# Giving the last unit's products banks of their own, folding the other sums in ahead, and writing the output through four banks

## The chip, the cores and the metric

One core of one Trainium2 chip. The metric is the device time of one execution in microseconds (us); the lower the better. The executions of the kernel before lie between 2330.62 and 2333.46 us, so they scatter by 2.8 us. TensorE, VectorE, ScalarE (ACT), GpSimd (POOL) and SyncE (SP) are the engines; SP issues all transfers of the output.

## The reference

```python
# x, f_logit: (4, 6080, 256); lower_bound: (256,)
f = lower_bound + (1 - lower_bound) * sigmoid(f_logit)
h = f[:, t] * h + (1 - f[:, t]) * x[:, t]      # for each t; y[:, t] = h
# y as (24320, 256); w_in (256, 2048), w_out (2048, 256)
h = y @ w_in
out = (h - tanh(h)) @ w_out
```

## The kernel before

The tokens run in blocks of 512, the hidden layer in four units of 512. Both matrix products use a seven-product scheme of the Strassen kind: in the second layer, the seven products of a unit accumulate over the units in four PSUM banks (pieces of the memory that TensorE writes its products to), Qa to Qd, and at the end of a block they are added up into the four quadrants C of the output. For all blocks but the last, that happens beside the next block's work. For the last there is nothing beside it, and its own routine `end` is used. The fast path is only valid for small values. It leaves a flag, and every engine reads the flag and branches around a general path.

```python
PARTS = (
    (("Qa", 0, A11, "h", 0), ("Qa", 1, S1, "T", 0)),
    (("Qb", 0, A12, "h", 3), ("Qb", 1, S2, "h", 1)),
    (("Qc", 0, S3, "T", 1),),
    (("Qd", 0, S4, "h", 2), ("Qd", 1, A22, "T", 2)),
)
...
def finish(j, step):          # p15 copies Qa; o1 to o4 add up C
...
    o, a, b = (
        None,
        (C[:, 0:2], acc[j, 1][:, :, 0:hb], twice(0)),
        (C[:, 2], acc[j, 2][:, 0, 0:hb], C[:, 1]),
        (C[:, 1:4:2], C[:, 1:3], twice(1)),
        (C[:, 1:3], acc[j, 3][:, :, 0:hb], C[:, 1:3]),
    )[step]
    nc.vector.tensor_tensor(out=o, in0=a, in1=b, op=ALU.add)
...
def end(j):                   # the last block, in place of o4
...
    for half in range(2):
        slot, r = ((2, 1), (1, 0))[half]
        nc.vector.tensor_tensor(
            out=C[:, slot], in0=acc[j, 3][:, r, 0:hb], in1=C[:, slot], op=ALU.add
        )
        name = ("Qa", "Qb")[half]
        bank = ps_b.tile([P, 2, KC, P], FP32, name=name, tag=name)
        for i in range(2):
            for k in range(KC):
                nc.tensor.transpose(
                    bank[:, i, k], C[:, 2 * k + half, i * P : (i + 1) * P], ident[:]
                )
        rows = osb[:, 2 * half : 2 * half + 2]
        (nc.scalar.copy, nc.vector.tensor_copy)[half](
            out=rows.rearrange("p i (m k) -> p i k m", k=KC), in_=bank[:]
        )
        t0 = starts[j] + half * hb
        nc.sync.dma_start(
            out=out[t0 : t0 + hb, :].rearrange("(i p) d -> p i d", p=P), in_=rows
        )
...
fast()
seen = nc.values_load(flag[:].bitcast(INT32), ...)
with tc.If(seen != 0):
    general()
```

Of the kernel before, what the change touches and what calls it, by code (L numbers as in the profile page):

```python
# [9 lines left out]
FP32 = mybir.dt.float32  # L10
ALU = mybir.AluOpType
# [6 lines left out]
P = 128  # L18
# [13 lines left out]
def kernel(  # L32
# [25 lines left out]
    nc = tc.nc  # L58

    B, S, D = x.shape  # L60
    DFF = moe_w_in.shape[1]
    N = B * S
    KC = D // P
    TB = 512
    HB = TB // 2
    NQ = TB // P
    NU = DFF // TB
# [6 lines left out]
    sizes = [HB] + [TB] * (N // TB)  # L74
    PLAIN, TURNED = 2, 2
    starts = [sum(sizes[:j]) for j in range(len(sizes))]
    NBLK = len(starts)
# [11 lines left out]
    ident = const.tile([P, P], FP32, name="ident")  # L89
# [156 lines left out]
    def fast(ctx):  # L246
# [11 lines left out]
        mixpool = ctx.enter_context(tc.tile_pool(name="mix", bufs=2))  # L258
# [6 lines left out]
        ps_a = ctx.enter_context(tc.tile_pool(name="ps_a", bufs=2, space=PSUM))  # L265
        ps_b = ctx.enter_context(tc.tile_pool(name="ps_b", bufs=1, space=PSUM))
# [4 lines left out]
        w_out = [wpool.tile([P, 7, 2 * P], FP32, name=f"w_out{u}") for u in range(NU)]  # L271
        A11, S3, A12, A22, S1, S2, S4 = range(7)
# [44 lines left out]
        def sum_weight(kind, u, s3):  # L317
            w = (w_in, w_out)[kind][u]
            A21 = S3
            sums = (  # L320
                (S1, A21, A22, ALU.add),
                (S2, S1, A11, ALU.subtract),
                (S4, A12, S2, ALU.subtract),
            )
            for o, a, b, op in ((S3, A11, A21, ALU.subtract),) if s3 else sums:
                nc.vector.tensor_tensor(
                    out=w[:, o, :], in0=w[:, a, :], in1=w[:, b, :], op=op
                )
# [126 lines left out]
        acc = {}  # L455

        def second_layer(n, part):


            j, u = units[n]  # L460
            products = PARTS[part]
            if u == 0:
                acc[j, part] = ps_b.tile([P, 2, HB], FP32, name=products[0][0])
            for c in range(2):
                for _, r, slot, right, q in products:
                    nc.tensor.matmul(  # L466
                        acc[j, part][:, r, 0 : st[n]["hb"]],
                        lhsT=w_out[u][:, slot, c * P : (c + 1) * P],
                        rhs=piece(n, right)[:, q, c],
                        start=(u == c == r == 0),  # L470
                        stop=(u == NU - 1 and c == 1),
                        skip_group_check=True,
                    )

        def finish(j, step):



            hb = sizes[j] // 2
            if step == 0:  # L480
                acc[j, "p"] = sumpool.tile([P, 2, HB], FP32, name="p15")
                nc.scalar.copy(out=acc[j, "p"][:, :, 0:hb], in_=acc[j, 0][:, :, 0:hb])
                return
            if step == 1:
                acc[j, "C"] = sumpool.tile([P, 4 * HB], FP32, name="C")
            C = acc[j, "C"][:, 0 : 4 * hb].rearrange("p (n t) -> p n t", n=4)

            def twice(i):
                return acc[j, "p"][:, i : i + 1, 0:hb].broadcast_to([P, 2, hb])
# [10 lines that stand above are left out]
        def give(j):  # L500
# [11 lines left out]
            for i in range(G):  # L512
# [2 lines left out]
                    in_=osb[i * H : (i + 1) * H, 0:n],  # L515
                )

        def end(j):


            hb = sizes[j] // 2
            C = acc[j, "C"][:, 0 : 4 * hb].rearrange("p (n t) -> p n t", n=4)
            osb = opool.tile([P, NQ, D], FP32, name="osb", tag="osb")
            for half in range(2):
                slot, r = ((2, 1), (1, 0))[half]
                nc.vector.tensor_tensor(
                    out=C[:, slot], in0=acc[j, 3][:, r, 0:hb], in1=C[:, slot], op=ALU.add
                )
                name = ("Qa", "Qb")[half]
                bank = ps_b.tile([P, 2, KC, P], FP32, name=name, tag=name)  # L530
                for i in range(2):
                    for k in range(KC):
                        nc.tensor.transpose(
                            bank[:, i, k], C[:, 2 * k + half, i * P : (i + 1) * P], ident[:]
                        )
                rows = osb[:, 2 * half : 2 * half + 2]
                (nc.scalar.copy, nc.vector.tensor_copy)[half](
                    out=rows.rearrange("p i (m k) -> p i k m", k=KC), in_=bank[:]
                )
                t0 = starts[j] + half * hb  # L540
                nc.sync.dma_start(
                    out=out[t0 : t0 + hb, :].rearrange("(i p) d -> p i d", p=P), in_=rows
                )

        steps.update(
# [14 lines left out]
            Qa=lambda n: second_layer(n, 0),  # L560
            Qb=lambda n: second_layer(n, 1),
            Qc=lambda n: second_layer(n, 2),
            Qd=lambda n: second_layer(n, 3),
# [6 lines left out]
            p15=lambda j: finish(j, 0),  # L570
            o1=lambda j: finish(j, 1),
            o2=lambda j: finish(j, 2),
            o3=lambda j: finish(j, 3),
            o4=lambda j: finish(j, 4),
            otr=give,
# [24 lines left out]
        for word in around.split():  # L600
            name, u, at = re.fullmatch(r"([a-zA-Z0-9]+)(?:\.(\d))?([+-]\d)?", word).groups()
# [156 lines left out]
        def p_give(j):  # L758
# [26 lines left out]
            A=lambda kind, u: sum_weight(kind, u, False),  # L785
            B=lambda kind, u: sum_weight(kind, u, True),
            F=p_first,
            t=p_square,
            q=p_quadratic,
            a=p_factor,  # L790
# [3 lines left out]
            o=p_give,  # L794
# [42 lines left out]
        def sum_up():  # L837

            most = ps_b.tile([P, 2, HB], FP32, name="most", tag="D")
            nc.tensor.matmul(  # L840
                most[0:1, 0, 0:1], lhsT=worst[:], rhs=ones[:], start=True, stop=True
            )
            nc.scalar.copy(out=flag[:], in_=most[0:1, 0, 0:1])
# [24 lines left out]
        def open_by(words):  # L868
            for word in words:
                name, *at = word.split(".")  # L870
                at = [int(i) for i in at]
                if name in opening:
                    opening[name](*at)
                else:
                    steps[name](at[0] * NU + at[1] if len(at) == 2 else at[0])

        with tc.manual_schedule():
            nc.vector.memset(zeros[:], 0.0)
            nc.vector.memset(ones[:], 1.0)
            nc.scalar.dma_start(  # L880
                out=lb[:], in_=lower_bound.rearrange("(p k) -> p k", k=KC)
            )
            make_identity(nc, ident[:])

            nc.scalar.activation(out=flag[:], in_=ones[0:1, :], func=AF.Sigmoid)
            nc.scalar.activation(
                out=om[:], in_=lb[:], func=AF.Identity, scale=-1.0, bias=1.0
            )
            nc.scalar.activation(out=nom[:], in_=lb[:], func=AF.Identity, bias=-1.0)
            busy = ps_b.tile([P, TB], FP32, name="B", tag="B")  # L890
            open_by(before.split())
            for cycle in range(PLAIN + 1, NBLK + 3):
                for name, u, at in turns:
                    j = cycle + at
                    if not PLAIN <= j < NBLK:
                        continue
                    if u is None:
                        if (name, j) == ("o1", NBLK - 1):
                            nc.vector.reduce_max(
                                out=worst[:], in_=flags[:], axis=mybir.AxisListType.X  # L900
                            )
                        if j == NBLK - 1 and name in ("o4", "otr"):
                            if name == "o4":
                                end(j)
                            continue
                        if (name, j) == ("o3", NBLK - 1):
                            sum_up()
                        steps[name](j)
                        if name == "tx" and j + 1 < NBLK:
                            fetch(j + 1)  # L910
                        continue
                    steps[name](j * NU + u)

    @with_exitstack
    def general(ctx):
# [15 lines left out]
        with tc.manual_schedule():  # L931
# [12 lines left out]
            for j, nb in enumerate(sizes):  # L944
# [57 lines left out]
                )  # L1002

    fast()
    seen = nc.values_load(
        flag[:].bitcast(INT32),
# [36 lines left out]
```

## Time and profile before

| | before |
|---|---|
| time, median of 3 runs (range) | 2332.53 us (2331.93 to 2333.46) |
| span of the profiled execution | 2329.3 us |
| end of TensorE's last product, by its pass's record | 2322.11 us |
| issues of the two output transfers | 2323.85 and 2324.43 us |
| last landing of the second | 2328.18 us |

The trace has 16 landings for each of these transfers; I take them as the reports of the 16 transfer engines that each write a part, and count the transfer as done with the last of them.

To compare ends of kernels, I count time in the rest of this document from one instruction that all of them have: the start of the one-column product `most`, which makes the flag. In the timeline of the kernel before it is this line (start, duration, engine, line, operation):

```profile
2319.99 0.19 PE L840 MATMUL most<-ones,worst 128*1 128x1 f32 x2
```

A time counted so is written with a plus sign. The span of the kernel before ends at +9.32.

### The profile page before, as it was taken

The numbers are of one execution on the slowest core, as the hardware profiler recorded it, in microseconds if no ns is written. First come the engines' busy times: TensorE is split into PE (matmuls) and PEld (weight loads), VectorE is DVE, ScalarE is ACT, GpSimd is POOL, SyncE is SP. The second block draws the span as 40 slices with busy tenths as digits, with TensorE's granted clock in tenths as the row PEclk, the third lists the DMA queues.
The fourth block names the chain that finished last, engine by engine and source line by source line (L and its number), as shares of the span: only waits on it lengthen the run. The fifth ranks groups of instructions, "written<-read, shape, count | busy, mean of one in ns | idle before, by whom it ended". The sixth has DMA issues, their size and how long they took to land.

```text
span 2329.3 us, 28648 instructions
## 1 busy us (share of the span) xinstructions
PE 2319.6 (100%) x10677; PEld 2025.2 (87%) x10677; DVE 2121.4 (91%) x2447; ACT 1801.1 (77%) x2686; POOL 0.7 (0%) x6
## 2 busy tenths in 40 slices
PE   9999999999999999999999999999999999999998
PEld 6888888888888888888888888888888888888887
DVE  8999899998999989999999999999899998999987
ACT  7677777777777777787777777777777777777775
POOL 0000000000000000000000000000000000000000
PEclk9999999999999999999999999999999999999999
DMA  6311211111111111112111121111211112111101
GB/s 172 64 24 32 42 37 28 28 35 39 37 28 28 37 36 37 28 28 42 32 37 28 28 45 28 37 28 28 46 29 36 28 28 46 31 33 28 28 10 29
DMA packets 296932, 85.05 MB, mean 37 GB/s; under 512 B 289872, under 2 KB 292688, under 8 KB 296784
## 3 DMA queue, kind: packets, MB, share of 16 engines
q1 hardware_dynamic: 296640, 83.14, 16.9%
q8 instruction: 85, 1.39, 0.2%
q14 instruction: 63, 0.52, 0.1%
q10 hardware_dynamic: 144, 0.00, 0.0%
HBM read 58.20 MB, written 24.90 MB: 36 GB/s over the span
## 4 chain that ended last, share of the span: by engine, by line
PE 99%; DMA 0%; SPq 0%; DVE 0%; issue 0%
PE A L383 27%; PE Qd L466 14%; PE Qa L466 14%; PE Qb L466 14%; PE D L383 14%; PE Qc L466 7%; PE B L383 7%; PE Qc L749 1%; PE Qb L749 1%; PE Qa L749 1%; PE A L682 1%; PE D L682 0%; PE Qd L682 0%; DMA xn<-in_x_dram 0%; PE B L682 0%; PE Qc L682 0%
## 5 line engine op out<-in xcount | busy, mean ns | idle before, releaser
L383 PE MATMUL A<-T,w_in 128*128 128x256 f32 x2208 | 558.8, 379 | 0.0
L383 PEld LDWEIGHTS A<-T,w_in 128*128 128x128 f32 x2208 | 419.5, 190 | 57.0
L427 DVE TENSOR_TENSOR h<-h,q 128x1024 f32<-128x1024 f32 x368 | 437.7, 1220 | 3.1
L421 DVE SCALAR_TENSOR_TENSOR q<-q,t 128x1024 f32<-128x1024 f32 x368 | 440.2, 1217 | 0.0
L414 ACT ACTIVATE q<-t 128x1024 f32<-128x1024 f32 x368 | 382.8, 1053 | 46.3 <-DVE h L427 43.4
L411 ACT ACTIVATE t<-h 128x1024 f32<-128x1024 f32 x368 | 388.7, 1057 | 3.1 <-DVE h L398 0.3
L432 ACT ACTIVATE junk<-t 128x1024 bf16<-128x1024 f32 x368 | 388.2, 1055 | 1.5
L446 DVE TENSOR_TENSOR Tg<-h 128x1024 f32<-128x1024 f32 x368 | 348.1, 946 | 6.4
L466 PE MATMUL Qb<-h,w_out 128*128 128x256 f32 x1472 | 347.7, 379 | 0.0
L466 PEld LDWEIGHTS Qb<-h,w_out 128*128 128x128 f32 x1472 | 279.7, 190 | 38.0
L466 PE MATMUL Qa<-Tg,w_out 128*128 128x256 f32 x736 | 219.0, 379 | 0.0
L466 PE MATMUL Qd<-h,w_out 128*128 128x256 f32 x736 | 219.0, 379 | 0.0
L466 PE MATMUL Qa<-h,w_out 128*128 128x256 f32 x736 | 218.9, 379 | 0.0
L466 PE MATMUL Qd<-Tg,w_out 128*128 128x256 f32 x736 | 218.9, 379 | 0.0
L395 ACT COPY h<-B 128x512 f32<-128x512 f32 x184 | 107.0, 582 | 143.2 <-PE B L383 94.4
L395 ACT COPY h<-A 128x512 f32<-128x512 f32 x184 | 107.3, 583 | 136.7 <-PE A L383 125.3
L398 DVE TENSOR_TENSOR h<-D,r 128x512 f32<-128x512 f32 x184 | 126.9, 690 | 92.9 <-PE D L383 90.8
L398 DVE TENSOR_TENSOR h<-A,r 128x512 f32<-128x512 f32 x184 | 126.3, 687 | 74.3 <-PE A L383 42.5
L395 ACT COPY r<-A 128x512 f32<-128x512 f32 x184 | 107.3, 583 | 105.9 <-PE A L383 105.9
L383 PE MATMUL D<-y,w_in 128*128 128x256 f32 x736 | 188.9, 379 | 0.0
L383 PE MATMUL B<-y,w_in 128*128 128x256 f32 x736 | 188.9, 379 | 0.0
L383 PE MATMUL A<-y,w_in 128*128 128x256 f32 x736 | 188.9, 379 | 0.0
(120 smaller groups left out, 3069.8 us busy)
## 6 DMA issues: line engine op xcount, KB each, us to landing
xn<-in_x_dram SPq DMA_DIRECT2D x184, 128.0 KB, 3.2
fn<-in_f_logit_dram SPq DMA_DIRECT2D x184, 128.0 KB, 3.1
out_dram<-osb SPq DMA_DIRECT2D x180, 128.0 KB, 2.8
raw<-in_moe_w_in_dram SPq DMA_DIRECT2D x8, 512.0 KB, 4.6
raw<-in_moe_w_out_dram SPq DMA_DIRECT2D x8, 512.0 KB, 4.8
out_dram<-osb SPq DMA_DIRECT2D x3, 256.0 KB, 3.7
fn<-in_f_logit_dram SPq DMA_DIRECT2D x1, 512.0 KB, 6.9
xn<-in_x_dram SPq DMA_DIRECT2D x1, 512.0 KB, 7.7
```

What stands on the lines that cost most here:

```text
L383: nc.tensor.matmul(ps[:, c], lhsT=w_in[u][:, slot, c * P : (c + 1) * P], rhs=mixes[j][right], start=start and c == 0, stop=True, skip_grou ...
L395: nc.scalar.copy(out=dst, in_=piece(n, bank))
L398: nc.vector.tensor_tensor(out=piece(n, "h")[:, q], in0=piece(n, bank), in1=piece(n, r), op=ALU.add)
L411: nc.scalar.activation(out=half(n, i, "t"), in_=half(n, i), func=AF.Square)
L414: nc.scalar.activation(out=half(n, i, "q"), in_=half(n, i, "t"), func=AF.Square, scale=RA, bias=RB,)
L421: nc.vector.scalar_tensor_tensor(out=q, in0=q, scalar=RC, in1=t, op0=ALU.add, op1=ALU.mult)
L427: nc.vector.tensor_tensor(out=h, in0=h, in1=q, op=ALU.mult)
L432: nc.scalar.activation(out=junk[:, :, :, 0 : st[n]["hb"]], in_=t, func=AF.Relu, bias=-TINY, accum_out=flags[:, 2 * n + i : 2 * n + i + 1],)
L446: nc.vector.tensor_tensor(out=o, in0=a, in1=b, op=ALU.subtract)
L466: nc.tensor.matmul(acc[j, part][:, r, 0 : st[n]["hb"]], lhsT=w_out[u][:, slot, c * P : (c + 1) * P], rhs=piece(n, right)[:, q, c], start=( ...
L682: nc.tensor.matmul(h[c], lhsT=w_in[u][:, 2 * k + s, c * P : (c + 1) * P], rhs=ys[j][:, k, 0:nb], start=k == 0 and (c == 0 or len(banks) == 2),
L749: nc.tensor.matmul(acc[j][i // 2][:, i % 2].rearrange("p (k m) -> p k m", k=2), lhsT=plain[j, u][:, s, c, i * P : (i + 1) * P], rhs=w_out[ ...
```

## The change

The intent: the last additions wait for all of Qd although each needs half of it (the first starts at 2322.14, Qd's last pass ends at 2322.11), and the copies and transfers wait for whole halves. In the kernel before, the passes (single runs of TensorE) of Qd's two products alternate. The change also puts the passes (single runs of TensorE) of each product together, the one that is needed first ahead. So the last unit's two Qd products go into banks of their own (`alone`), what Qd holds of the other three units is copied out early and folded into C ahead (`kept`), and each half of the output passes through two banks, which ACT and VectorE copy at the same time.

```diff
--- before.py
+++ after.py
@@ -515,31 +515,67 @@
                     in_=osb[i * H : (i + 1) * H, 0:n],
                 )
 
+        def part_end(j, step):
+            hb = sizes[j] // 2
+            p, kept = acc[j, "p"][:, :, 0:hb], acc[j, "kept"]
+            if step == "o1":
+                finish(j, 1)
+            if step == "p15":
+                nc.vector.tensor_tensor(
+                    out=kept[:, 2], in0=p[:, 1], in1=kept[:, 0], op=ALU.add
+                )
+                return
+            C = acc[j, "C"][:, 0 : 4 * hb].rearrange("p (n t) -> p n t", n=4)
+            for o, a, b in {
+                "o1": (),
+                "o2": ((kept[:, 3], acc[j, 2][:, 0, 0:hb], C[:, 1]),),
+                "o3": (
+                    (C[:, 2], kept[:, 3], kept[:, 1]),
+                    (C[:, 1], C[:, 1], kept[:, 2]),
+                    (C[:, 3], kept[:, 3], p[:, 1]),
+                ),
+            }[step]:
+                nc.vector.tensor_tensor(out=o, in0=a, in1=b, op=ALU.add)
         def end(j):
 
 
-            hb = sizes[j] // 2
+            hb, n = sizes[j] // 2, j * NU + NU - 1
             C = acc[j, "C"][:, 0 : 4 * hb].rearrange("p (n t) -> p n t", n=4)
             osb = opool.tile([P, NQ, D], FP32, name="osb", tag="osb")
+            alone = [ps_a.tile([P, TB], FP32, name="A", tag="A")[:, 0:hb] for _ in range(2)]
+            for half, (slot, right, q) in enumerate(((A22, "T", 2), (S4, "h", 2))):
+                for c in range(2):
+                    nc.tensor.matmul(
+                        alone[half],
+                        lhsT=w_out[NU - 1][:, slot, c * P : (c + 1) * P],
+                        rhs=piece(n, right)[:, q, c],
+                        start=c == 0,
+                        stop=c == 1,
+                    )
             for half in range(2):
-                slot, r = ((2, 1), (1, 0))[half]
+                slot = 2 - half
                 nc.vector.tensor_tensor(
-                    out=C[:, slot], in0=acc[j, 3][:, r, 0:hb], in1=C[:, slot], op=ALU.add
-                )
-                name = ("Qa", "Qb")[half]
-                bank = ps_b.tile([P, 2, KC, P], FP32, name=name, tag=name)
+                    out=C[:, slot], in0=alone[half], in1=C[:, slot], op=ALU.add
+                )
                 for i in range(2):
-                    for k in range(KC):
+                    name = ("Qa", "Qb", "Qc", "D")[2 * half + i]
+                    bank = ps_b.tile([P, KC, P], FP32, name=name, tag=name)
+                    for k in (0, 1) if half == 0 else (1, 0):
                         nc.tensor.transpose(
-                            bank[:, i, k], C[:, 2 * k + half, i * P : (i + 1) * P], ident[:]
+                            bank[:, k], C[:, 2 * k + half, i * P : (i + 1) * P], ident[:]
                         )
-                rows = osb[:, 2 * half : 2 * half + 2]
-                (nc.scalar.copy, nc.vector.tensor_copy)[half](
-                    out=rows.rearrange("p i (m k) -> p i k m", k=KC), in_=bank[:]
-                )
+                    (nc.scalar.copy, nc.vector.tensor_copy)[i](
+                        out=osb[:, 2 * half + i].rearrange("p (m k) -> p k m", k=KC),
+                        in_=bank[:],
+                    )
                 t0 = starts[j] + half * hb
                 nc.sync.dma_start(
-                    out=out[t0 : t0 + hb, :].rearrange("(i p) d -> p i d", p=P), in_=rows
+                    out=out[t0 : t0 + hb, :].rearrange("(i p) d -> p i d", p=P),
+                    in_=osb[:, 2 * half : 2 * half + 2],
                 )
 
         steps.update(
@@ -894,22 +930,35 @@
                     j = cycle + at
                     if not PLAIN <= j < NBLK:
                         continue
+                    final = j == NBLK - 1
+                    if final and (name, u) == ("Qd", NU - 1):
+                        continue
                     if u is None:
-                        if (name, j) == ("o1", NBLK - 1):
+                        if final and name == "o1":
                             nc.vector.reduce_max(
                                 out=worst[:], in_=flags[:], axis=mybir.AxisListType.X
                             )
-                        if j == NBLK - 1 and name in ("o4", "otr"):
-                            if name == "o4":
-                                end(j)
+                        if final and name == "o3":
+                            sum_up()
+                        if final and name == "o4":
+                            end(j)
+                        if final and name[0] == "o":
+                            if name in ("o1", "o2", "o3"):
+                                part_end(j, name)
                             continue
-                        if (name, j) == ("o3", NBLK - 1):
-                            sum_up()
                         steps[name](j)
                         if name == "tx" and j + 1 < NBLK:
                             fetch(j + 1)
+                        if final and name == "p15":
+                            part_end(j, name)
                         continue
                     steps[name](j * NU + u)
+                    if final and (name, u) == ("Qd", NU - 2):
+                        kept = mixpool.tile([P, 4, HB], FP32, name="T")
+                        acc[j, "kept"] = kept
+                        nc.scalar.copy(
+                            out=kept[:, 0:2], in_=acc[j, 3][:, :, 0 : sizes[j] // 2]
+                        )
 
     @with_exitstack
     def general(ctx):
```

## The prediction

> **What bounds the kernel now.** I read the page's busy times first, then the chain of work that ended last, then the timeline of the last ten microseconds, because the diff touches only the last block.
>
> ```profile
> PE 2319.6 (100%) x10677; PEld 2025.2 (87%) x10677; DVE 2121.4 (91%) x2447; ACT 1801.1 (77%) x2686; POOL 0.7 (0%) x6
> PE 99%; DMA 0%; SPq 0%; DVE 0%; issue 0%
> ```
>
> TensorE is busy for the whole span and makes 99% of the chain. A change of a few instructions can only matter where TensorE has nothing left to do, which is after its last product. The chain in order of time shows where that is:
>
> ```profile
> 2317.47 1.73 PE Qb L466 x8
> 2319.20 0.86 PE Qc L466 x4
> 2320.06 0.12 PE most L840 x2
> 2320.18 1.94 PE Qd L466 x8
> 2322.14 0.43 DVE C L526
> 2322.62 0.55 PE Qa L533 x3
> 2323.17 0.52 PE Qb L533 x4
> 2323.71 0.69 DVE osb L537
> ```
>
> The last products (Qd, eight passes of 0.216 us) end at 2322.11. Then come, one after another, an addition, seven transposes, a copy of 512 columns and the output transfers. The span is 2329.3, so everything after the last product is 7.2 us, 0.3% of it. That is the ceiling of any gain here, and most of it is not compute: the transfers and the end of the program take the last 4.9 us. The timeline:
>
> ```profile
> 2320.56 0.69 DVE L498 TENSOR_TENSOR C<-C,p 128x512 f32<-128x512 f32 x1
> 2322.14 0.76 DVE L526 TENSOR_TENSOR C<-Qd,C 128x256 f32<-128x256 f32 x2 [0.89 <-PE Qd L466]
> 2322.62 0.55 PE L533 MATMUL Qa<-ident,C 128*128 128x128 f32 x3 [0.41 <-DVE C L526]
> 2323.21 0.61 ACT L537 COPY osb<-Qa 128x512 f32<-128x512 f32 x1 [2.84 <-PE Qa L533]
> 2323.71 0.69 DVE L537 COPY osb<-Qb 128x512 f32<-128x512 f32 x1 [0.81 <-PE Qb L533]
> 2323.85 0.97 SPq L541 DMA_DIRECT2D out_dram<-osb  x2
> ```
>
> The reader is to see that VectorE idles 0.89 us for Qd, TensorE then 0.41 us for VectorE, and that the two transfers go out at 2323.85 and 2324.43 (two issues of 0.39 within 0.97). The lines of the output transfers and of the branch at the program's end say what follows:
>
> ```profile
> DMA to landing us min/median/max: 3.7/3.7/3.8
> L1009 PEldq COMPARE_BRANCH  x1: 3711/3711/3711, 2323.7 to 2323.7; - x1
> L1009 DVEq EVENT_SEMAPHORE  x1: 21/21/21, 2327.6 to 2327.6; - x1
> ```
>
> So the second transfer lands at 2324.43 + 3.75 = 2328.18, and 1.14 us later the span ends. TensorE takes 3.71 us to get past the branch around the general path, until 2327.37, and VectorE resumes at 2327.6: these are 0.6 us behind the landing, not far. The landings of the two transfers show one thing more. On 15 of the 16 engines the first transfer has landed by 2326.59 and the second by 2327.56, most of them by 2325.95 and 2326.70; one engine is last for both, at 2327.57 and 2328.18. Instruction fetches (two of 8 KB at 2324.60 and 2324.66, one of 16 KB at 2324.71 that takes 1.24 us) run just as the output packets start, and that straggler is what sets the end.
>
> [...]the addition that needs only half of Qd starts at 2322.14, after all eight passes (2322.11). This is why the change gives each product its own bank.[...] The trace has 424 and 691 or 692 for the additions of C. So splitting an operation in two costs a fixed part again; though two independent ones overlap (L526 starts at 2322.145 and 2322.486, 0.34 apart).[...]
>
> **The change, part by part.** The instruction orders of the two kernels differ in nothing but the last block's end.
>
> First, the sums. The copy of Qd after the third unit (ACT, 512 columns, about 0.57 us) lands in the 5.20 us in which ACT waits for Qa, and the addition of kept and p (0.42 us on VectorE) in the gap of 0.72 us before L498 at 2319.30. Both are hidden: 0. The fold-in then puts three additions of 256 columns in the place of one of 512: started at 2320.56, then 2320.90 and 2321.24. The first needed addition of the last product follows at 2321.58, where the old one started at 2322.14, provided its product is ready. It is: the first product's four passes take the place of the first four of Qd and end at 2321.24.
>
> Second, the transposes. The addition ends at 2322.00. TensorE does the other product until 2321.94, so it meets the finished C with hardly a wait: Qa's second transpose at 2322.06 (before 2322.62), Qb's two at 2322.22 and 2322.33 (0.165 after the first, then 0.109, as in the trace). TensorE work is the same: eight passes and eight transposes.
>
> Third, the copies, now of 256 columns in four banks. ACT copies Qa from 2322.42 for 0.40 (L762 has 0.40 for such a copy). VectorE copies Qb from 2322.64 to 2323.06. The first transfer is issued at **2323.09, 0.76 us earlier** than 2323.85.
>
> Fourth, the second half, and here is the catch. In VectorE's order the second addition stands behind the copy of Qb, though its product is ready at 2322.11. It starts at 2322.64 + 0.34 = 2322.98 and ends at 2323.40. The last transposes of Qc and D follow at 2323.45, 2323.61 and 2323.72, end at 2323.99, and VectorE's copy of D runs 2324.03 to 2324.45. The second transfer is issued at **2324.47, against 2324.43 before: 0.04 us later.** What the copies' halving wins (0.27 us) and what the early addition wins is spent in VectorE's queue.
>
> Fifth, the landing. The first transfer's 16 KB per engine takes 16 packets of 46 ns, 0.74 us, so it leaves the engines before about 2324.8, when the second's packets are not yet there. The straggler then carries only one output transfer behind the fetches. The branches move later by 0.3 to 0.6 us with the last waits of each engine, so the fetches still meet the second transfer. If the straggler spends 1.36 us on fetches (2324.60 to 2325.96) from about 2325.0 and then 0.74 on the packets, it is done at 2327.1, against 2327.77 before, and lands at about 2327.5. But TensorE and VectorE come out of the branch at about 2327.8, 0.4 us later than before with some of it given back by freer engines. The later of the two, near 2327.8, stands against 2328.18.
>
> The sum: 0 (hidden sums) + 0.04 (issue) − 0.44 (landing, limited by the fetches) = −0.4 us. From 2332.53 this makes **2332.1 us**.
>
> **The rivals.** (a) The full gain: 0.76 us, if the second half followed the first as it does on ACT. Against it stands VectorE's order. It would make 2331.8. (b) No gain: the second issue is where it was, and if the straggler owes its delay to fetches alone, which move later with the branches, the landing stays or slips by 0.3 us. It would make 2332.5 to 2332.8.[...] (c) VectorE becomes the bound of the end earlier: three additions end at 2321.66 instead of 2321.25. The old addition waited until 2322.14 in any case, so this has 0.5 us of slack; I give it little. (d) A wait on another bank, say of a transpose for the copy of the flag (2320.37) or of the kept sums, is long over and costs nothing.
>
> **Range and chances.** All rivals lie within 1 us, 0.04% of the time. The three runs before span 1.5 us, which is larger than the effect, so the range is mostly noise: 2331.1 to 2333.1. A change of 2% would be 47 us, and the whole part that the diff touches lasts about 10 us, so within 2% is nearly certain.
>
> **What would show each step right or wrong.** The timeline after should show: the first addition of the last product near 2321.6; no wait of TensorE above 0.15 us before Qa's second transpose; the first issue near 2323.1 and the second near 2324.5; the second addition starting after the copy of Qb, not at 2322.14; landing of the second transfer 3.0 to 3.4 us after its issue instead of 3.75. I am wrong if the second issue comes before 2324.0 (then VectorE's order did not bind), if the second transfer still takes 3.7 us or more to land (rival b), or if TensorE shows a new wait before its last products.

## The result, and the profile after

| | before | changed |
|---|---|---|
| time, median of 6 runs (range) | 2332.3 us (2331.25 to 2333.46) | 2332.8 us (2331.64 to 2333.39) |
| ratio | 1 | 1.0001 (95% interval 0.9988 to 1.0014) |
| span of the profiled execution | 2329.3 us | 2330.3 us |
| first, second issue of output | +3.85, +4.44 | +3.43, +4.52 |
| TensorE reaches the branch, gets past it | +3.66, +7.37 | +4.04, +8.31 |
| last landing of the second transfer | +8.19 | +8.46 |
| end of the span | +9.32 | +9.59 |

A ratio here is the mean time of one kernel's runs over that of the other's of the same rounds, so it is not quite the ratio of the medians.

The profiled span is 1.0 us longer, but most of that is not the end of the kernel. The product `most` starts at 2320.74 instead of 2319.99, and up to the last products the two kernels have the same instructions in the same order on every engine but for two early sums (a copy on ACT and an addition on VectorE). The difference is there in the first 20 us. From the view of stretches, TensorE alone, before and then changed (stretch, its length, TensorE busy, instructions, granted clock, share of the transfer engines, GB/s):

```profile
0.00:10.00 10.00, 6.83 (x19) 1.00 0.79 255
10.00:20.00 10.00, 9.53 (x44) 1.00 1.17 292
```

```profile
0.00:10.00 10.00, 6.67 (x19) 1.00 0.77 236
10.00:20.00 10.00, 8.78 (x43) 1.00 1.12 291
```

TensorE is busy 16.36 us of them before and 15.45 after. In the fourteen profiles `most` starts anywhere from 2319.80 to 2322.33, with no visible relation to what was changed at the end. The changed kernel's two profiles show what this does to the time: of the 1.26 us between their spans, 0.94 lies before `most` and 0.32 after it.

The end itself, from the timeline of the changed kernel:

```profile
2320.74 0.19 PE L876 MATMUL most<-ones,worst 128*1 128x1 f32 x2
...
2321.31 0.42 DVE L541 TENSOR_TENSOR C<-T 128x256 f32<-128x256 f32 x1
...
2322.32 0.42 DVE L561 TENSOR_TENSOR C<-A,C 128x256 f32<-128x256 f32 x1
...
2323.16 0.38 ACT L571 COPY osb<-Qa 128x256 f32<-128x256 f32 x1 [2.04 <-PE Qa L568]
...
2323.38 0.42 DVE L571 COPY osb<-Qb 128x256 f32<-128x256 f32 x1 [0.64 <-PE Qb L568]
2323.72 0.41 DVE L561 TENSOR_TENSOR C<-A,C 128x256 f32<-128x256 f32 x1
2324.17 1.48 SPq L576 DMA_DIRECT2D out_dram<-osb  x2
...
2324.19 0.33 PE L568 MATMUL Qc<-ident,C 128*128 128x128 f32 x1 [0.74 <-DVE C L561]
...
2324.78 0.42 DVE L571 COPY osb<-D 128x256 f32<-128x256 f32 x1 [0.64 <-PE D L568]
```

The first addition starts at +1.58 (2322.32 minus 2320.74) instead of +2.15, as intended. The second starts at +2.98 instead of +2.49, because in VectorE's order it stands behind the copy of Qb, and that waits 0.64 us for TensorE. TensorE in turn waits 0.74 us for the second addition. The two issues of the output, 0.39 us each, stand 1.09 apart within the 1.48 of their line. The chain of waits of the changed kernel names the same step, between VectorE's copy and the last transposes:

```profile
2323.38 0.42 DVE osb L571
2323.80 0.34 DVE C L561
2324.14 0.04 issue
2324.19 0.33 PE Qc L568
```

And this is what follows the issues, from the lines of the transfers and of the branch in the changed kernel:

```profile
DMA to landing us min/median/max: 2.8/3.4/3.9
L1058 PEldq COMPARE_BRANCH  x1: 4267/4267/4267, 2324.8 to 2324.8; - x1
L1058 DVEq EVENT_SEMAPHORE  x1: 21/21/21, 2329.0 to 2329.0; - x1
```

The first transfer now lands 2.8 us after its issue (3.7 before), but the second needs 3.9 instead of 3.75, and TensorE's branch comes 0.4 us later and takes 4.27 us instead of 3.71.

### The profile page after: what moved, and what is told of

It is laid out like the page before. It is cut to its first block, busy times and chain, and to the rows that moved or that the text cites. A ratio compares the mean times of both kernels' runs of the same rounds, so it can differ in the third digit from the quotient of the medians. Undisturbed runs are those within 1.5% of the kernel's fastest.

```text
span 2330.3 us, 28654 instructions
## 1 busy us (share of the span) xinstructions
PE 2319.4 (100%) x10677; PEld 2025.3 (87%) x10677; DVE 2122.1 (91%) x2451; ACT 1802.2 (77%) x2688; POOL 0.7 (0%) x6
## 4 chain that ended last, share of the span: by engine, by line
PE 99%; DMA 0%; SPq 0%; DVE 0%; issue 0%
PE A L383 27%; PE Qa L466 14%; PE Qb L466 14%; PE D L383 14%; PE Qd L466 14%; PE B L383 7%; PE Qc L466 7%; PE Qa L785 1%; PE Qb L785 1%; PE Qc L785 1%; PE A L718 1%; PE D L718 0%; PE Qd L718 0%; DMA xn<-in_x_dram 0%; PE B L718 0%; PE A L552 0%
## 5 line engine op out<-in xcount | busy, mean ns | idle before, releaser
L383 PE MATMUL D<-T,w_in 128*128 128x256 f32 x736 | 188.9, 379 | 0.0
```

The costliest lines, as they stand in the source:

```text
L383: nc.tensor.matmul(ps[:, c], lhsT=w_in[u][:, slot, c * P : (c + 1) * P], rhs=mixes[j][right], start=start and c == 0, stop=True, skip_grou ...
```

## The experiments

The theories. **Q**: VectorE's queue order holds the second half back. **D**: the end follows the issue of the second output transfer. **F**: the end follows the branch, whose instruction fetches (packets of the kind "instruction" in the trace) hold up one engine of the output transfers and the engines that take the branch. Line numbers differ from kernel to kernel by a few. All twelve runs were correct.

| run | issues | TensorE at and past branch | last landing | end | ratio to before (interval) |
|---|---|---|---|---|---|
| before | +3.85, +4.44 | +3.66, +7.37 | +8.19 | +9.32 | 1 |
| before_again | +3.86, +4.44 | +3.67, +7.32 | +8.13 | +9.27 | 0.9999 (0.9979 to 1.0019) |
| changed | +3.43, +4.52 | +4.04, +8.31 | +8.46 | +9.59 | 1.0001 (0.9988 to 1.0014) |
| after_again | +3.43, +4.52 | +4.04, +7.83 | +7.98 | +9.27 | 0.9999 (0.9983 to 1.0016) |
| add_first | +3.42, +3.93 | +3.22, +7.23 | +8.08 | +9.21 | 0.9993 (0.9976 to 1.0010) |
| two_banks | +3.29, +4.05 | +3.23, +7.70 | +8.52 | +9.65 | 0.9998 (0.9982 to 1.0015) |
| four_banks_only | +4.00, +5.10 | +4.62, +8.85 | +9.08 | +10.21 | 1.0001 (0.9984 to 1.0017) |
| per_half | +3.11, +3.78 | +3.23, +7.62 | +8.44 | +9.57 | 0.9999 (0.9983 to 1.0016) |
| before_late_branch | +3.86, +4.44 | +5.36, +9.28 | +7.57 | +10.40 | 1.0004 (0.9988 to 1.0021) |
| before_late_transfer | +3.86, +5.16 | +3.67, +8.08 | +8.77 | +10.01 | 1.0008 (0.9991 to 1.0025) |
| before_nobranch | +3.85, +4.44 | none | +6.79 | +7.80 | 0.9995 (0.9978 to 1.0012) |
| after_nobranch | +3.43, +4.52 | none | +6.67 | +7.69 | 0.9994 (0.9977 to 1.0010) |
| add_first_nobranch | +3.42, +3.93 | none | +6.34 | +7.36 | 0.9993 (0.9977 to 1.0010) |
| per_half_nobranch | +3.11, +3.78 | none | +6.04 | +7.06 | 0.9990 (0.9973 to 1.0007) |

No total time is clear of noise: every interval holds 1. What follows is read from the traces, mostly one profile for each kernel, and a difference of less than 0.3 us at the end is not counted, since the changed kernel's two profiles differ by that (+9.59 and +9.27).

### How far the ends repeat

The changed kernel and the kernel before once more, with no edit.

> The changed kernel once more, for how far the profile of the end repeats. Second transfer issued at +4.52 (plus or minus 0.05, it is a fixed chain of compute), its landing and the end within 0.3 us of +8.46 and +9.59. The first transfer is issued 0.33 us after VectorE's copy of the second bank has ended; whether this repeats is open. The opening (time of 'most' from the start of the span, 2319.99 before and 2320.74 in the changed kernel) should scatter by about 0.7 us, as the two kernels are the same there.

> The kernel before once more, for how far its end repeats. Counted from 'most': issues at +3.85 and +4.44, TensorE's branch at +3.66 (all within 0.02); the 16 KB fetch at about +4.7, TensorE past the branch within 0.4 us of +7.37, last landing within 0.4 us of +8.19, end within 0.4 us of +9.32. If the end lies as far as 0.3 us off, the two kernels' ends (9.32, and 9.59 or 9.27) are not apart.

The compute repeats to 0.01 us: issues at +3.43 and +4.52, at +3.86 and +4.44. What comes after the issues repeats less well. In the changed kernel the last landing is 0.48 us earlier in the second profile and the end 0.32 us earlier, both outside the expected 0.3. So the two kernels' ends, +9.32 and +9.27 against +9.59 and +9.27, are not apart, and the 0.27 us that the first pair of profiles showed is not a loss that one may explain.

### Part by part: add_first, two_banks, four_banks_only

add_first moves one statement of the changed kernel:

```diff
             for half in range(2):
                 slot = 2 - half
                 nc.vector.tensor_tensor(
                     out=C[:, slot], in0=alone[half], in1=C[:, slot], op=ALU.add
                 )
+            for half in range(2):
                 for i in range(2):
```

> The change with its second addition put ahead of VectorE's copies, nothing else. All times here are counted from the start of the one-column product 'most', which stands 9.32 us before the end of the span in the kernel before and 9.59 us in the changed one. Theory Q (VectorE's queue order holds the second half): the second addition starts when its product is done, at +2.15 instead of +2.98, and the second transfer is issued at +3.65 to +3.9 instead of +4.52. Theory F (the end follows TensorE's branch around the general path, 5.55 to 5.66 us after it): the branch comes at about +3.2 instead of +4.04, so the end at about +8.8. Theory D (the end follows the issue of the second transfer by 4.9 to 5.1 us): the end at +8.6 to +9.0. If neither the order nor the branch binds, the end stays at +9.3 to +9.6. In total time within 1 us of before: same.

Its VectorE timeline (`most` at 2321.46):

```profile
2323.61 0.42 DVE L561 TENSOR_TENSOR C<-A,C 128x256 f32<-128x256 f32 x1 [0.16 <-PE A L552]
2324.10 0.42 DVE L572 COPY osb<-Qb 128x256 f32<-128x256 f32 x1
2324.68 0.42 DVE L572 COPY osb<-D 128x256 f32<-128x256 f32 x1 [0.16 <-PE D L569]
```

The second addition starts at +2.15, when its product is done, and the second transfer goes out at +3.93 instead of +4.52. Q holds: the order cost 0.6 us of the issue. The expected +3.65 to +3.9 was missed by a little: VectorE's last copy ended at +3.64, but SP was busy with the first issue until +3.81. TensorE comes to the branch at +3.22, as expected. But the end, expected at +8.6 to +9.0 by D and +8.8 by F, is at +9.21. Neither simple rule holds: the issue 0.6 us earlier brought almost nothing.

two_banks puts the output of the changed kernel back to two banks:

```diff
-                    name = ("Qa", "Qb", "Qc", "D")[2 * half + i]
-                    bank = ps_b.tile([P, KC, P], FP32, name=name, tag=name)
+                name = ("Qa", "Qb")[half]
+                bank = ps_b.tile([P, 2, KC, P], FP32, name=name, tag=name)
... (transposes, copies and transfers as in the kernel before)
```

> One part undone: sums folded ahead and the products in banks of their own stay, the output goes back to two banks with copies of 512 columns, so that no copy stands between VectorE's two additions. Counted from the start of 'most': second addition at +2.15, second transfer issued at +4.0 (a 0.69 us copy from +3.28), TensorE's branch at +3.2. Theory Q: the second issue is earlier than in the kernel before (+4.44) and in the changed one (+4.52), so the four banks are what cost the gain. F: end at +8.8. D: end at +9.0. If the folding ahead itself is worthless, issue at +4.4.

Its second issue is at +4.05, 0.39 us ahead of the kernel before and 0.47 ahead of the full change: without a copy between them, the two additions run at +1.58 and +2.15. Its end is at +9.65, no better, where F had said +8.8 and D +9.0.

four_banks_only takes the kernel before and writes its output through four banks, as the change does, with the sums and products as they were.

> One part alone: the kernel before with the output in four banks of 256 columns, its sums and products as they were. Counted from the start of 'most': first addition at +2.15, the second behind the copy of the second bank at about +3.5 (before: +2.49), second transfer issued at about +5.0, TensorE's branch at about +4.6. Theory Q says worse than both kernels; F: end at +10.2; D: end at +10.0. If the four banks help by halving the copies, the issue comes at +4.2.

Its second addition starts at +3.56, and VectorE's timeline shows why (`most` at 2320.28):

```profile
2323.50 0.42 DVE L536 COPY osb<-Qb 128x256 f32<-128x256 f32 x1 [0.64 <-PE Qb L533]
2323.84 0.41 DVE L526 TENSOR_TENSOR C<-Qd,C 128x256 f32<-128x256 f32 x1
```

The second issue is at +5.10, 0.66 us later than before. The parts do not simply add up. The early sums and own banks win 0.39 us of the second issue with two banks (+4.44 to +4.05) and 0.58 with four (+5.10 to +4.52). The four banks, in the order that the change has, cost 0.66 us alone and 0.47 together with the rest, so the whole change loses 0.08. The early sums, the own banks and the new order of the passes were not run apart. The end, at +10.21, is where F had it (+10.2; D said +10.0) and 0.9 us later than before, the only one of the four that is clearly worse (two_banks, 0.33 later, is at the edge of the scatter).

### Without the branch: before_nobranch, after_nobranch, add_first_nobranch

The same edit in each, for the question only: the result is right for this input, but the guard for large values is gone.

```diff
     fast()
-    seen = nc.values_load(...)
-    with tc.If(seen != 0):
-        general()
```

> The kernel before without the branch to the general path and the read of the flag (right for this input, not a version to use). Counted from 'most', the second transfer is still issued at +4.44. Theory F (instruction fetches after the branch share one transfer engine with the output and make the straggler): no engine's landing lags; all 16 land within 0.3 us of each other at about +7.0, the end at about +8.1 instead of +9.32, and total time 1 to 2 us less. Theory D (the output transfer itself needs 3.75 us): landing at +8.19, end at +9.3.

> The changed kernel without the branch. Second issue at +4.52 as with it. F: landing of all 16 engines at about +6.9 (15 of the 16 landed by +7.02 and +7.07 in its two profiles), end at +8.0 instead of +9.59 and +9.27; so the same as before without the branch within 0.15 us, which would mean that the change wins nothing even where no fetch disturbs. D: +8.5 and +9.6.

> The change with the second addition ahead of the copies, without the branch. Second issue at +3.93 as with the branch. If without fetches the end follows the issue (3.36 us behind it in the kernel before without the branch, 3.17 in the changed one), the end is at +7.1 to +7.3, 0.5 us or more ahead of both (+7.80 and +7.69). If the landings are bound by something else, it stays at +7.7.

The lines of the output transfers of before_nobranch and then of after_nobranch:

```profile
L541 SPq DMA_DIRECT2D out_dram<-osb x2: 389/389/389, 2325.3 to 2325.9; - x2
...
DMA to landing us min/median/max: 2.2/2.3/2.4
```

```profile
L576 SPq DMA_DIRECT2D out_dram<-osb x2: 389/389/389, 2324.9 to 2326.0; - x2
...
DMA to landing us min/median/max: 2.1/2.2/2.3
```

The issues stand where they stood, and the transfers land 2.1 to 2.4 us after them, where the same kernels with the branch have 2.8 to 4.7. The straggler (the engine that lands last by far) is gone: in before_nobranch 15 of the 16 engines have landed by +6.75 and the last at +6.79; with the branch it was +7.57 and +8.19. The ends are at +7.80 and +7.69, even earlier than F's +8.1 and +8.0: the branch, with the reads of the flag and the fetches that go with it, costs the kernel before 1.5 us. And these two ends are only 0.11 us apart, so even without the branch the change as it stands wins nothing clear; its second issue is no earlier than before. The times agree, if they are pooled: the sixteen executions of the four kernels without the branch average 2330.0 us, the fourteen of the kernel before in the same rounds 2331.8, with a standard error of 0.3 for the difference. And now the end does follow the issue: 3.36, 3.17, 3.43 and (per_half_nobranch) 3.28 us behind it in the four kernels without a branch. The end of add_first_nobranch, +7.36, is 0.33 us ahead of the changed kernel without the branch. That is a little later than the expected +7.1 to +7.3, less than the 0.59 us by which its issue is earlier, and hardly above the scatter. per_half_nobranch, below, shows the worth of an earlier issue more clearly.

### Only the branch later, only the transfer later

before_late_branch gives TensorE one more transpose, of what VectorE copied last, into a bank that nobody reads:

```diff
+            spare = ps_b.tile([P, P], FP32, name="Qc", tag="Qc")
+            nc.tensor.transpose(spare[:], osb[:, 3, 0:P], ident[:])
```

> The kernel before with one more transpose on TensorE at the very end, whose operand is VectorE's last copy and whose result nobody reads: TensorE comes to the branch at about +5.05 instead of +3.66, transfers are issued as before (+3.85, +4.44). F (the end follows TensorE's branch by 5.6 us): end at about +10.6, TensorE past the branch at about +9.2. D (the end follows the transfers): end stays at +9.3. Middle: if the fetch then comes after the output packets have gone, transfers land by +7.0 and only the fetch itself sets the end.

The lines of its branch (kind of duration: min, median, max in ns; first and last start):

```profile
L1011 PEldq COMPARE_BRANCH  x1: 3927/3927/3927, 2325.2 to 2325.2; - x1
...
L1011 PEldq EVENT_SEMAPHORE  x1: 51/51/51, 2329.2 to 2329.2; - x1
```

The transfers are issued as before, and the end moves from +9.32 to +10.40 (F had said +10.6). D is refuted as the whole story: the transfers landed at +7.57 already, earlier than in the kernel before, and TensorE was still behind the branch until +9.28. The 16 KB fetch began at +6.40, 1.05 us after TensorE's branch (1.02 to 1.06 in the kernel before, add_first, two_banks and per_half, but 1.26 to 1.92 in the other kernels with the branch), and in every run TensorE was released 1.3 to 1.5 us after that fetch ended. The landings say more: with only TensorE's branch and that fetch moved, the first transfer landed at +6.59 instead of +7.57 and the second at +7.57 instead of +8.19. Without any branch the second landed at +6.79. So the time of this fetch makes some 0.6 of the 1.4 us that the branch adds to the second landing; the rest stays with what else belongs to the branch.

before_late_transfer does VectorE's last copy twice.

> The kernel before with VectorE's last copy done twice: the second transfer is issued 0.7 us later, at about +5.16, TensorE's branch stays at +3.66 (VectorE's own branch moves from +4.34 to +5.05). D: end 0.7 us later, at +10.0. F: the end stays within 0.3 us of +9.3, as the fetch of 16 KB holds the slow engine in any case.

The end moves by 0.7 us, to +10.01, the number that D gave. But the run does not separate the two: VectorE's branch moved too, from +4.34 to +5.38, the fetch of 16 KB came at +5.59 instead of +4.72, and VectorE was through its branch at +8.93, 0.16 us after the last landing. I count it as inconclusive.

### A version without the wait of two engines: per_half

The first transfer of the changed kernel is issued 0.36 us after the copy that it waited for (VectorE's copy ends at +3.06). It waits for two engines, and in the trace the wait for VectorE is an instruction of its own ahead of the transfer, 3.29 us long (17 ns for those of per_half). per_half is add_first with each half copied by one engine:

```diff
-                    (nc.scalar.copy, nc.vector.tensor_copy)[i](
+                    (nc.scalar.copy, nc.vector.tensor_copy)[half](
```

> The change with the second addition first, and each half's two copies on one engine: ACT does both banks of the first half, VectorE both of the second, so that each transfer waits for one engine and needs no separate wait instruction with two semaphores. If that separate instruction costs the 0.33 us between VectorE's copy (+3.06) and the first issue (+3.42), the first transfer goes out at +3.2, within 0.05 us of the end of ACT's second copy, and the second at +3.8. If the 0.33 us is of another origin, the first issue stays 0.3 us behind the copy. With the branch the end stays between +8.9 and +9.6, as the fetch of TensorE (branch at +3.22) meets the output packets in any case.

> The same without the branch: second issue at +3.8, end at +7.0 to +7.2, so 0.5 to 0.7 us ahead of the changed kernel without the branch (+7.69): the whole that the change could have won, if no fetch disturbed its end.

From the timelines of per_half, ACT and then SP, and the landings, with the branch and then without:

```profile
2324.14 0.39 ACT L572 COPY osb<-Qb 128x256 f32<-128x256 f32 x1
```

```profile
2324.56 1.06 SPq L577 DMA_DIRECT2D out_dram<-osb  x2
```

```profile
DMA to landing us min/median/max: 4.7/4.7/4.7
```

```profile
DMA to landing us min/median/max: 2.2/2.2/2.3
```

ACT's copy ends at +3.08 and the first issue is at +3.11, 0.03 behind it. Over all runs: where the last wait stands in the transfer itself (the kernel before, also late or without the branch, two_banks, per_half) the first issue follows the copy by 0.02 to 0.03 us; where it stands in a wait instruction ahead (the changed kernel, add_first, four_banks_only, and those of them that were run again or without the branch) by 0.36. The second transfer, whose wait instruction waited 0.6 us at most, shows no such delay. Why a long wait there costs 0.33 us, these runs do not show.

per_half_nobranch ends at +7.06, as expected and 0.63 us ahead of the changed kernel without the branch. With the branch it ends at +9.57. Its second transfer is issued 0.74 us earlier than in the changed kernel and lands at +8.44, no earlier than there (+8.46 and +7.98): 4.7 us after its issue. This is the clearest pair. I had looked for a version that beats both kernels; with the branch in place none of these does so clear of the scatter.

## Why the prediction was right or wrong

The range held: 2332.8 us against 2331.1 to 2333.1. That says nothing for the mechanism: the range was set by the noise, and both rivals that have a number, 2331.8 and 2332.5 to 2332.8, lie in it too. The predicted gain of 0.4 us did not come; by its own steps:

- **The sums are hidden: right.** The first needed addition stood at 2321.58 minus 2319.99 = +1.59 in the prediction and at +1.58 in the trace. No wait was added ahead of TensorE's last products.
- **The transposes: right.** Predicted +2.07, +2.23 and +2.34; measured +2.06, +2.22 and +2.33.
- **The first issue: wrong by a missing term.** Predicted +3.10, measured +3.43. The copies came as computed (+2.42 and +2.64), but the wait instruction ahead of the transfer added 0.33 us. This did not delay the second issue of the changed kernel, which waits for the copy of D (until +4.46); in add_first it did.
- **The second half behind the copy of Qb: right**, and it is the main reason why the compute side won nothing. Second addition +2.99 predicted, +2.98 measured; second issue +4.48 and +4.52. add_first shows it as the cause: one statement moved, and the issue came 0.6 us earlier.
- **The landing: wrong.** The step that failed is the fifth. Its first half held: "The straggler then carries only one output transfer behind the fetches"; the first transfer had landed at +6.19 and +6.31. What failed is the time of the second: fetches from about 2325.0 for 1.36 us, then 0.74 us of packets, and the landing at about 2327.5, which is +7.5. Measured: +8.46 and +7.98. The 16 KB fetch ended at +6.83 and +6.42 instead of about +6.37, and the 16 late packets of the second transfer took 1.17 and 1.05 us, the first six of them 0.09 to 0.14 us each instead of 0.046. Together these are 0.9 and 0.4 us. Rival (b) had named the later fetch. In the changed kernel TensorE's branch came at +4.04 instead of +3.66, the 16 KB fetch at +5.61 instead of +4.72. The prediction's own sign of being wrong, "3.7 us or more to land", came true in the first profile (3.94) and not in the second (3.46). The term "−0.44 (landing)" is 0 within the scatter.
- **Slips in the working.** The −0.44 is derived nowhere: 2327.8 against 2328.18 is −0.38, with the issue already in it. TensorE and VectorE left the branch 0.8 and 0.6 us ahead of the landing, not behind it. And the addition at 2322.14 does not show that the bank was waited for: its half of Qd was complete only with the last pass (2322.11), as the passes of the two products alternate.

So where did the gain go? On the compute side, into VectorE's order: add_first and two_banks bring the second issue 0.5 to 0.6 us forward of the changed kernel's. And what a better order frees is swallowed after the issue, by what the branch brings with it. That the branch causes the straggler is shown by the runs without it; they take out its fetches and the reads of the flag together. That the 16 KB fetch has a part in it is shown by before_late_branch. That it occupies the same transfer engine is an inference: the records of packets do not name the engine, but in the changed kernel, after_again and four_banks_only the last 16 packets begin within 0.01 us of the end of the 16 KB fetch (in the first, 2327.565 and 2327.569). With the branch, the end comes 1.0 to 1.2 us after the later of two things in every kernel here, the last landing or the last engine out of the branch. That both hang on the fetches fits all runs but is not shown for each.

## What to carry to other kernels

Before shaving work at the end of a program, take the end apart into issue, landing and what the engines do after their last instruction; here the part after the last issue was two thirds (4.9 of 7.2 us), and per_half, whose second transfer went out 0.74 us earlier than the changed kernel's, ended no earlier. When operations are split over more banks, write down the order that each engine's queue then has: here a copy put between two additions cost more of the second issue than the halved copies won. A branch around a rarely used path need not be free, here 1.5 us: try the kernel once without it to see what it costs.

## What the traces show of the branch, a long wait and two additions

- Here the fetch of 16 KB took 1.0 to 2.1 us (1.24 in the kernel before, 1.21 in the changed one), TensorE stood 3.65 to 4.47 us in its branch, and output transfers that land in 2.1 to 2.4 us without the branch needed up to 4.7 with it.
- The records of the branch have 45 to 72 ns on four engines, and 3.65 to 4.47 us on TensorE. A short record is not the whole cost either: in the kernel before, VectorE's took 72 ns, and its next instruction came 3.2 us later.
- The first transfer, where it stood behind a wait instruction of its own that waited long (3.29 us in the changed kernel), was issued 0.33 us late: 0.36 us after the copy, against 0.03 where the wait stands in the transfer.
- Two VectorE additions of 256 columns started 0.46 us apart where the second needs the first (+0.11 and +0.57 in the changed kernel), against 0.34 where the two are independent (+0.57 and +0.91).
